# Three unused gaps in on-chip memory: moving every stationary operand of two MLP layers to the same place modulo 512 bytes

## The chip, the cores and the metric

The kernel runs on one core of a Trainium2 chip. The metric is device time in microseconds (us), and the figure given for a kernel is the median of its runs. A profile is one more execution, recorded by the hardware profiler; its time is its span, from the first instruction to the last.

The engines carry short names in the profile: PE is the matrix engine's multiplication, PEld its loading of weights (the stationary operand of a matmul, 128 rows by 128 columns, which must sit in the array before the moving operand, up to 512 columns, streams past it), DVE the vector engine, ACT the scalar engine, POOL the third elementwise engine, and SP the queue from which nearly all transfers (DMAs) are issued. SBUF is the on-chip memory of 128 partitions; an address below is the byte offset inside each partition.

## The reference: what is computed

Four layers are applied to x of 2048 tokens by 1024 channels, in float32: a convolution layer A, an MLP layer B, then A and B once more with the same weights.

```python
x = A_q
x = x + _A_ref(_layernorm(x), A_k, A_v, A_shift_k, A_ssm_k, A_ssm_D)
x = x + _B_ref(_layernorm(x), B_w1, B_b1, B_w2, B_b2)
x = x + _A_ref(_layernorm(x), A_k, A_v, A_shift_k, A_ssm_k, A_ssm_D)
x = x + _B_ref(_layernorm(x), B_w1, B_b1, B_w2, B_b2)
# _A_ref: k is convolved with 4 taps, multiplied by v, convolved causally with
#         a filter of 2048 taps per channel (by FFT in the reference), times q
# _B_ref: h = relu(x @ w1 + b1) ** 2      (1024 -> 3584)
#         h @ w2 + b2                     (3584 -> 1024)
```

The convolution's factor does not depend on x, so it is computed once and used in both A layers.

## The kernel before, in words

**Arithmetic.** An MLP product is made of three matmuls with operands split in a high and a low part (`mm3`, lines 334 to 337): high by high (L335), high by low (L336), low by high (L337), the first operand being the stationary one and the second the moving one. In the profile an instruction's inputs are named moving first: `p<-xh,whl` streams `xh` past weights `whl`.

**Tiling.** The 2048 tokens form 4 blocks of 512. A unit is one block in one MLP layer, eight in all, in the order of `ORDER`. Each unit has two kinds of matmul steps:

- m1 (first product): the stationary operand is a 128 by 128 piece of w1, in a tile `whl` (two parts of 512 columns), and the moving operand is the transposed, normalised block, `xh` and `xl`. A unit holds 28 hidden blocks of 128 by 8 input blocks by 3, which is 672 matmuls of 512 columns; at the seams of some units the block is taken in two halves of 256 columns.
- m2 (second product): the roles turn. The stationary operand is the activated hidden value, `rh` and `rl`, 128 of its 512 tokens at a time; the moving operand is a piece of w2 in `whl`. Units 0 to 4 have 28 hidden blocks by 2 halves of the output by 4 token tiles by 3, which is 672 such matmuls a unit.

In the last three units (`WINO`, units 5 to 7) the second product is done by a scheme with seven instead of eight products for each 2 by 2 group of blocks (4 token halves and weight blocks combined). Of its seven, three still take `rh` and `rl` as stationary operand (14 pairs by 3 by 2 by 3, 252 matmuls a unit), and four take sums of activations held in the tiles `cx`, `cg` (high parts), `cp`, `fy` (low parts) (14 by 4 by 2 by 3, 336 a unit). These four are called z below.

**Order of the work.** The order on each engine is written out by hand, step by step. Each step of the main loop (from `for s, (k, u, c, a, i, tts, w)` on) advances the ring of weights (`w_advance`: raw tiles `wr` loaded up to 8 steps ahead, the high part cast by ACT at L1012, the low part by DVE or POOL at L1020, or a split pair loaded ready-made from DRAM as `whl<-wd_m`), issues the matmuls, and then lets a share of the convolution's work (`prod_stream`, the product at L525 and its reduction at L529) and the preparation of the next unit run. The first block's convolution and normalisation are ordered ahead of that by a small planner (`first_block`). All of this depends on tiles and their buffers, not on addresses.

**Where the tiles lie.** Pools of SBUF lie end to end in the order in which they are opened: `const`, `cv`, `pre`, `mw`, `ml`. In a pool, names take their places in the order of first use, and each buffer is rounded up to a multiple of 32 bytes. This gives, for the kernel before:

| pool | tiles | byte address of the first | modulo 512 |
|---|---|---|---|
| const | ident, fh, fl, ih, il | 16512, then 17024, 19072, 21120, 22144 | 128 |
| cv | fx (4 buffers of 2080 bytes) | 23392 | 352, 384, 416, 448 |
| cv | yh, fg, cx, cg, cp, fk, sm, fy, yl | yh at 31712, cx at 41952, cp at 58336 | 480 |
| pre | px and small ones | px at 92096 | 448 (px) |
| mw | xh, xl, wr, whl | xh at 100736, whl at 149888 | 384 |
| ml | b1t | 174464 | 384 |
| ml | rh, rl, acc, yt | rh at 174592, rl at 190976 | 0 |

A 128 by 128 float32 piece takes 512 bytes of a partition, and the slices of `whl`, `rh`, `rl` and the z tiles start at whole multiples of 512 bytes within their tile. So in m1 stationary and moving operand both start at 384 modulo 512; in m2 the moving one starts at 384 and the stationary one at 0; in z it is 384 and 480. The prologue's pool `pro` lies where `ml` comes to lie later. The last byte used is at 227840.

Of the kernel before, what the change touches and what calls it, by code (L numbers as in the profile page):

```python
# [10 lines left out]
F32 = mybir.dt.float32  # L11
# [8 lines left out]
P = 128  # L20
# [4 lines left out]
FT = F // P  # L25
# [215 lines left out]
def tile_h3_mlp(ctx: ExitStack, tc: tile.TileContext, q, kT, vT, shk, ssmT, ssmD, w1, b1, w2, b2,  # L241
# [5 lines left out]
    dram = ctx.enter_context(tc.tile_pool(name="dram", bufs=1, space=DRAM))  # L247
    const = ctx.enter_context(tc.tile_pool(name="const", bufs=1))
    cv = ctx.enter_context(tc.tile_pool(name="cv", bufs=1))
    pre = ctx.enter_context(tc.tile_pool(name="pre", bufs=1))  # L250
    ps = ctx.enter_context(tc.tile_pool(name="ps", bufs=1, space=PSUM))
    ctx.enter_context(tc.manual_schedule())
# [800 lines left out]
            w_lo()  # L1053

    mw = ctx.enter_context(tc.tile_pool(name="mw", bufs=1))
    rs = {}

    def first_block():
# [423 lines left out]
    xT = first_block()  # L1482
    pds = prod_stream()
    ml = ctx.enter_context(tc.tile_pool(name="ml", bufs=1, reuse_waits="tile"))
    b1t = ml.tile([P, FT], F32, name="b1t", bufs=1)
    SY.dma_start(b1t, b1)
    lag = slag
    soon, behind = Later(), Later()
# [493 lines left out]
```

## Time and profile before

| | |
|---|---|
| three runs | 2735.21, 2728.89, 2734.58 us; median 2734.58 us |
| profiled execution, its span | 2729.8 us |
| granted PE clock in it, mean | 0.997 |
| PE busy | 2685.5 us, 98% |
| PE weight load busy | 2230.2 us, 82% |
| DVE / ACT / POOL busy | 1994.4 / 1124.3 / 844.6 us |
| DMA packets, share of 16 engines | 80.3% |

A busy time is the union of an engine's instructions. A matmul's record lasts longer than the distance to the next one's start, because matmuls are pipelined and their ends are modelled; so the mean duration of a record says less than the distance between starts. That distance is read from a stretch of time that holds only one kind of matmul: its length divided by their number. In a list of stretches, the number in brackets after a busy time counts every instruction that overlaps the stretch, so that one or two may reach in from before.

### The profile page before, as it was taken

The page shows a single profiled execution, that of the slowest core. Times are in us where ns is not written, and L with a number is a line of the kernel's source. Part 1 is how long each engine was busy: PE and PEld are TensorE (multiplying, and loading weights), DVE is VectorE, ACT ScalarE, POOL GpSimd, SP SyncE. Part 2 cuts the span into 40 slices and gives each one's busy share as a digit, 9 for nine tenths or more (in the row PEclk, how much of TensorE's full clock was granted, in tenths as well). Part 3 has the DMA queues.
Part 4 walks back from the last instruction along what each step waited for, and adds up shares of the span by engine and source line. Part 5 has one row for each costly group of instructions (what it writes and reads, how often), then busy time and mean ns, then how long its engine had stood idle before and what let it go on. Part 6 is the DMA issues. An engine that isn't in the chain of part 4 may idle for free.

```text
span 2729.8 us, 36533 instructions
## 1 busy us (share of the span) xinstructions
PE 2685.5 (98%) x12568; PEld 2230.2 (82%) x12568; DVE 1994.4 (73%) x3066; ACT 1124.3 (41%) x1936; POOL 844.6 (31%) x532
## 2 busy tenths in 40 slices
PE   7999999999999999999999999999999999999999
PEld 7888787888888888888888888888788788888887
DVE  7878888788987878779677655366787666664565
ACT  3454344434444233442234422244455444445443
POOL 2436564445532645236553454000100010001000
PEclk9999999999999999999999999999999999999999
DMA  7789898699989898888977887788888766685546
GB/s 251 263 299 318 288 316 290 213 312 374 322 297 326 293 338 276 273 330 286 348 259 270 300 296 251 228 287 311 304 281 299 275 230 212 223 282 198 177 166 204
DMA packets 377482, 755.05 MB, mean 277 GB/s; under 512 B 43840, under 2 KB 159184, under 8 KB 377296
## 3 DMA queue, kind: packets, MB, share of 16 engines
q1 hardware_dynamic: 377296, 752.72, 80.3%
q8 instruction: 99, 1.62, 0.3%
q14 instruction: 87, 0.71, 0.1%
HBM read 602.63 MB, written 149.95 MB: 276 GB/s over the span
## 4 chain that ended last, share of the span: by engine, by line
PE 80%; DMA 9%; DVE 5%; POOL 2%; issue 2%; SPq 1%; ACT 1%; DVEq 0%; POOLq 0%; ACTq 0%
PE p L336 24%; PE p L337 24%; PE p L335 24%; PE p L1095 2%; DMA wr<-w 2%; DMA cg<-gd 1%; DMA whl<-wd_m 1%; DVE whl L1020 1%; PE pt L335 1%; PE pt L337 1%; PE pt L336 1%; POOL cp L525 1%; DMA wd_m<-whl 1%; DMA wd_t<-whl 0%; DMA fg<-ssmT 0%
## 5 line engine op out<-in xcount | busy, mean ns | idle before, releaser
L525 POOL TENSOR_TENSOR cp<-cx,cg 128x384 f32<-128x384 f32 (+5 forms) x288 | 541.5, 1892 | 580.1 <-DVE sm L529 394.4
L335 PE MATMUL p<-xh,whl 128*128 128x512 f32 (+1 forms) x1840 | 706.7, 384 | 2.2 <-DMA whl<-wd_m 2.2
L337 PE MATMUL p<-xh,whl 128*128 128x512 f32 (+1 forms) x1840 | 703.5, 382 | 0.8 <-POOL whl L1020 0.8
L336 PE MATMUL p<-xl,whl 128*128 128x512 f32 (+1 forms) x1840 | 702.8, 382 | 0.1
L1012 ACT CAST whl<-wr 128x512 fp32r<-128x512 f32 x637 | 383.5, 619 | 445.9 <-PE p L337 270.2
L335 PE MATMUL p<-whl,rh 128*128 128x512 f32 x1372 | 548.1, 399 | 5.4 <-ACT whl L1012 3.6
L1020 DVE TENSOR_TENSOR whl<-wr,whl 128x512 fp32r<-128x512 f32 x622 | 499.4, 823 | 73.1 <-ACT whl L1012 65.0
L336 PE MATMUL p<-whl,rh 128*128 128x512 f32 x1372 | 543.8, 396 | 2.0 <-DVE whl L1020 1.1
L337 PE MATMUL p<-whl,rl 128*128 128x512 f32 x1372 | 543.0, 396 | 0.0
L335 PEld LDWEIGHTS p<-xh,whl 128*128 128x128 f32 x1840 | 346.2, 188 | 69.7 <-DVE acc L1606 1.8
L337 PEld LDWEIGHTS p<-xh,whl 128*128 128x128 f32 x1840 | 345.9, 188 | 68.7 <-POOL whl L1020 1.0
L336 PEld LDWEIGHTS p<-xl,whl 128*128 128x128 f32 x1840 | 346.0, 188 | 66.1 <-DVE xl L1408 0.3
L335 PEld LDWEIGHTS p<-whl,rh 128*128 128x128 f32 x1372 | 259.5, 189 | 65.8 <-ACT whl L1012 4.5
L336 PEld LDWEIGHTS p<-whl,rh 128*128 128x128 f32 x1372 | 259.6, 189 | 62.3 <-DVE whl L1020 3.3
L337 PEld LDWEIGHTS p<-whl,rl 128*128 128x128 f32 x1372 | 259.3, 189 | 60.5
L1502 DVE TENSOR_TENSOR rl<-wr,rh 128x512 fp32r<-128x512 f32 x140 | 143.3, 1024 | 181.6 <-ACT rh L1497 181.5
L1599 POOL TENSOR_TENSOR acc<-acc,px 128x512 f32<-128x512 f32 x18 | 23.1, 1321 | 771.2 <-DMA px<-b 771.2
L529 DVE TENSOR_REDUCE sm<-cp 128x128 f32<-128x384 f32 (+5 forms) x288 | 249.3, 874 | 9.3 <-POOL cp L525 9.3
L1494 ACT ACTIVATE wr<-p,b1t 128x512 f32<-128x512 f32 x138 | 95.3, 690 | 376.9 <-PE p L337 373.6
L1563 DVE TENSOR_TENSOR rl<-wr,rh 128x256 fp32r<-128x256 f32 x84 | 50.0, 596 | 209.4 <-ACT rh L1558 209.2
L1622 DVE TENSOR_TENSOR acc<-p,acc 128x512 f32<-128x512 f32 x152 | 101.5, 687 | 87.0 <-PE p L337 86.6
L1555 ACT ACTIVATE wr<-p,b1t 128x512 f32<-128x512 f32 x84 | 57.9, 689 | 189.8 <-PE p L337 187.9
(277 smaller groups left out, 3319.9 us busy)
## 6 DMA issues: line engine op xcount, KB each, us to landing
whl<-wd_m SPq DMA_DIRECT2D x379, 512.0 KB, 5.2
wr<-w SPq DMA_DIRECT2D x493, 256.0 KB, 5.3
wr<-td SPq DMA_DIRECT2D x152, 256.0 KB, 4.1
wd_m<-whl SPq DMA_DIRECT2D x70, 512.0 KB, 6.0
cx<-xd SPq DMA_DIRECT2D x48, 512.0 KB, 6.0
cg<-gd SPq DMA_DIRECT2D x48, 512.0 KB, 6.7
gd<-fg SPq DMA_DIRECT2D x72, 256.0 KB, 6.2
cx<-xd SPq DMA_DIRECT2D x48, 384.0 KB, 5.5
```

Source lines behind the costliest of these rows:

```text
L335: PE.matmul(o, lh, rh, start=start, stop=False)
L336: PE.matmul(o, lh, rl, start=False, stop=False)
L337: PE.matmul(o, ll, rh, start=False, stop=stop)
L525: G.tensor_mul(pr.rearrange("p c i -> p i c"), xt[:, 0:j + 1], gt[:, j::-1])
L529: V.tensor_reduce(sm[:, ty, jj], st["pr"], axis=AX.X, op=OP.add)
L1012: A.copy(t[:, 0], raws[n]["t"])
L1020: ENG[e[n % len(e)]].tensor_sub(t[:, 1], raws[n]["t"], t[:, 0].bitcast(F32))
L1095: PE.matmul(o, lh, r, start=start, stop=stop)
L1494: A.activation(r, st["o"], AF.Relu, bias=b1t[:, st["f"]:st["f"] + 1])
L1502: V.tensor_sub(st["lo"], st["r"]["t"], st["hi"].bitcast(F32))
L1555: A.activation(r, st["o"], AF.Relu, bias=b1t[:, st["f"]:st["f"] + 1])
L1622: V.tensor_add(accs[tt][:, d], o, accs[tt][:, d])
```

## The change

Three places take up room that nothing uses: a tile `gap` of 104 float32 (416 bytes) as the first of pool `cv`, a tile `gapm` of 24 float32 (96 bytes) as the first of pool `mw`, and 96 further float32 (384 bytes) behind `b1t`, the first tile of pool `ml`, which is then used through a slice of its old width.

```diff
     cv = ctx.enter_context(tc.tile_pool(name="cv", bufs=1))
+    cv.tile([P, 104], F32, name="gap", bufs=1)
     pre = ctx.enter_context(tc.tile_pool(name="pre", bufs=1))
...
     mw = ctx.enter_context(tc.tile_pool(name="mw", bufs=1))
+    mw.tile([P, 24], F32, name="gapm", bufs=1)
     rs = {}
...
     ml = ctx.enter_context(tc.tile_pool(name="ml", bufs=1, reuse_waits="tile"))
-    b1t = ml.tile([P, FT], F32, name="b1t", bufs=1)
+    b1t = ml.tile([P, FT + 96], F32, name="b1t", bufs=1)[:, 0:FT]
     SY.dma_start(b1t, b1)
```

The addresses follow. Pools `cv` and `pre` move up by 416 bytes: the `cv` tiles from 480 to 384 modulo 512, `fx` to 256, 288, 320 and 352, `px` to 352. Pool `mw` moves by 416 + 96 = 512 bytes and stays at 384. Pool `ml` begins 512 bytes higher, still at 384; `b1t` used to take 128 bytes and now takes 512 (496 rounded up), so `rh`, `rl`, `acc` and `yt` go from 0 to 384. After it the stationary and the moving operands of m1, m2 and z all start at 384 modulo 512. The last byte used is at 228736. No instruction, wait or transfer is added, removed or put elsewhere in the order.

## The prediction, on record before the result

> **What bounds the kernel now.** I read the page of the profile first: shares, slices, chain.
>
> ```profile
> span 2729.8 us, 36533 instructions
> PE 2685.5 (98%) x12568; PEld 2230.2 (82%) x12568; DVE 1994.4 (73%) x3066; ACT 1124.3 (41%) x1936; POOL 844.6 (31%) x532
> ...
> DMA  7789898699989898888977887788888766685546
> ...
> PE 80%; DMA 9%; DVE 5%; POOL 2%; issue 2%; SPq 1%; ACT 1%; DVEq 0%; POOLq 0%; ACTq 0%
> ```
>
> PE is busy for 98% of the span and carries 80% of the chain that ended last. A share of 98% still says nothing about how fast PE goes while busy, so I went on to the groups of PE instructions with shapes kept apart. The name before the comma is the moving operand, the one behind it the stationary one.
>
> ```profile
> L335 PE MATMUL p<-xh,whl 128*128 128x512 f32 x1712 | 670.0, 391 | 2.2 <-DMA whl<-wd_m 2.2
> L337 PE MATMUL p<-xh,whl 128*128 128x512 f32 x1712 | 667.1, 390 | 0.0
> L336 PE MATMUL p<-xl,whl 128*128 128x512 f32 x1712 | 666.5, 389 | 0.0
> L335 PE MATMUL p<-whl,rh 128*128 128x512 f32 x1372 | 548.1, 399 | 5.4 <-ACT whl L1012 3.6 <-DMA whl<-wd_m 1.6
> L336 PE MATMUL p<-whl,rh 128*128 128x512 f32 x1372 | 543.8, 396 | 2.0 <-DVE whl L1020 1.1 <-POOL whl L1020 0.9
> L337 PE MATMUL p<-whl,rl 128*128 128x512 f32 x1372 | 543.0, 396 | 0.0
> L337 PE MATMUL p<-whl,cp 128*128 128x512 f32 x264 | 104.6, 396 | 0.0
> L335 PE MATMUL p<-whl,cg 128*128 128x512 f32 x168 | 67.0, 399 | 0.3 <-DMA whl<-wd_t 0.3
> L335 PE MATMUL p<-whl,cx 128*128 128x512 f32 x168 | 66.8, 397 | 0.0
> L336 PE MATMUL p<-whl,cg 128*128 128x512 f32 x168 | 66.7, 397 | 0.3 <-DVE whl L1020 0.3
> L336 PE MATMUL p<-whl,cx 128*128 128x512 f32 x168 | 66.6, 396 | 0.0
> L337 PE MATMUL p<-whl,fy 128*128 128x512 f32 x72 | 28.5, 396 | 0.0
> ```
>
> All twelve groups are the same instruction: 128 rows by 128 columns, 512 columns moving. Yet m1 (the first three) lasts 389 to 391 ns and m2 and z last 396 to 399. The counts are m1 5136, m2 3 x 1372 = 4116, z 264 + 4 x 168 + 72 = 1008. The records overlap, so I look for the distance between starts. In the list of instructions in order of time I took the first matmul of a run of one kind and the first of the next kind, and in the list of stretches exactly what lies between:
>
> ```profile
> 1642.51 0.40 PE L335 MATMUL p<-whl,rh 128*128 128x512 f32 x1
> ...
> 1662.03 0.39 PE L335 MATMUL p<-xh,whl 128*128 128x512 f32 x1
> ...
> 2028.81 0.39 PE L335 MATMUL p<-whl,cx 128*128 128x512 f32 x1
> ...
> 2051.30 0.39 PE L335 MATMUL p<-xh,whl 128*128 128x512 f32 x1
> ...
> 2094.83 0.40 PE L335 MATMUL p<-whl,rh 128*128 128x512 f32 x1
> ```
>
> ```profile
> core 0: us, PE busy (x) PEld busy (x) DVE busy (x) ACT busy (x) POOL busy (x), PEclk, DMA share, GB/s
> 2051.30:2094.83 43.53, 43.53 (x193) 36.05 (x192) 32.34 (x68) 21.07 (x35) 0.00 (x0) 1.00 0.90 305
> 1642.51:1662.03 19.52, 19.52 (x86) 15.83 (x85) 16.76 (x18) 3.38 (x7) 14.92 (x8) 1.00 0.79 287
> 2028.81:2051.30 22.49, 22.49 (x97) 18.08 (x96) 17.41 (x32) 8.59 (x14) 0.00 (x0) 1.00 0.85 287
> ```
>
> By the code these stretches hold 8 hidden blocks of m1 (8 x 8 x 3 = 192 matmuls), one output half of seven hidden blocks of m2 (7 x 4 x 3 = 84), and four pairs of z (4 x 4 x 2 x 3 = 96). So a matmul takes 43.53 / 192 = 226.7 ns in m1, 19.52 / 84 = 232.4 ns in m2 and 22.49 / 96 = 234.3 ns in z, each with PE busy to the last hundredth and the granted clock at 1.00. No wait explains the difference; each rate is PE's own.
>
> What differs? m2 and z have the same moving tile `whl` and the same step of three matmuls, and still differ by 1.9 ns; what separates them is the stationary tile, at 0 modulo 512 in m2 and at 480 in z. m1 has it at 384, the place of its moving operand. Three places, three rates. The slices of `whl` and `rh` run through every multiple of 512 bytes, so a longer period than 512 is not what the rows ask for.
>
> **The change part by part.** No instruction is added, so every term is a change of duration.
>
> *The tiles `rh` and `rl` go from 0 to 384 (gap behind `b1t`).* If what sets the rate is the start of the stationary operand modulo 512, taken alone or against the moving operand at 384, m2 becomes what m1 is: 232.4 - 226.7 = 5.7 ns less, times 4116, 23.4 us. I take this value because m1's row is the nearest: the same instruction with both operands at 384. The other end is no gain, 0; a loss is weighed under the rivals.
>
> *The z tiles go from 480 to 384 (gap in `cv`).* 234.3 - 226.7 = 7.6 ns less, times 1008, 7.7 us; other end 0.
>
> *The gap in `mw`* gains nothing by itself: with the one in `cv` it makes 512 and keeps `whl`, `xh`, `xl` at 384. m1, 0 us.
>
> Sum if PE sets the end throughout: 31.1 us. How much of it reaches the end is seen from PE's idle time by region:
>
> ```profile
> 0.00:546.00 546.00, 512.45 (x2730) 441.60 (x2731) 447.58 (x686) 238.38 (x422) 258.89 (x202) 0.98 0.84 280
> 546.00:1843.00 1297.00, 1294.67 (x6000) 1073.26 (x5999) 972.49 (x1338) 471.04 (x831) 555.06 (x307) 1.00 0.86 298
> 1843.00:2729.80 886.80, 878.39 (x3842) 715.34 (x3840) 574.31 (x1044) 414.86 (x684) 30.61 (x24) 1.00 0.71 243
> 570.00:720.00 150.00, 148.50 (x703) 123.89 (x702) 135.01 (x170) 58.83 (x106) 84.66 (x50) 1.00 1.00 351
> ```
>
> Up to 546 us (prologue and unit 0, with 672 m2) PE is idle for 33.6 us: others end there. Of unit 0's 672 x 5.7 = 3.8 us I count half, because I cannot say which of its steps wait; the bounds are 0 and 3.8. From 546 to 1843 us (units 1 to 4, 2688 m2, 15.3 us of gain) PE is idle for 2.3 us in 1297, so the gain goes through. The one warning is 570 to 720 us, where the DMA share is 1.00: there transfers cannot come any faster, and about 150 / 1297 of 2688 m2, 311 of them worth 1.8 us, may give half of it back. From 1843 us on (756 m2 worth 4.3 us, z worth 7.7 us) PE is idle for 8.4 us of 887 and the DMA share is 0.71: all of it counts. The cover for the rest is DVE, whose busy share between 546 and 1843 us is 972 / 1297 = 75%; 1.2% less time makes it 76%. If that cover were gone, the 15.3 us would be. The stretch with the least room is again 570 to 720 us, DVE 135 of 150.
>
> So 31.1 - 1.9 - 0.9 = 28.3 us.
>
> *What else moves.* These rows price it.
>
> ```profile
> L335 PE MATMUL p<-xh,whl 128*128 128x256 f32 x128 | 36.7, 287 | 0.0
> L335 PE MATMUL pt<-fg,fh 128*128 128x256 f32 x64 | 18.2, 284 | 1.5 <-DVE fy L403 1.5
> L336 PE MATMUL pt<-fx,fh 128*128 128x256 f32 x64 | 18.0, 281 | 0.0
> L1012 ACT CAST whl<-wr 128x512 fp32r<-128x512 f32 x637 | 383.5, 619 | 445.9 <-PE p L337 270.2 <-DMA wr<-w 46.3 <-DVE acc L1606 34.9
> L1497 ACT CAST rh<-wr 128x512 fp32r<-128x512 f32 x140 | 87.0, 622 | 4.5
> acc<-x SPq DMA_DIRECT2D x25, 512.0 KB, 7.2
> px<-x SPq DMA_DIRECT2D x32, 512.0 KB, 6.0
> ```
>
> The convolution's matmuls of 256 columns (576 of them, stationary `fh`, `fl`, `ih`, `il` at 128) see their moving tiles go from 480 (or `fx`, 352 to 448) to 384 (256 to 352). The known rows of this shape lie between 281 and 287 ns at three pairs of places, so each may change by 6 ns either way: 576 x 6 = 3.5 us, either sign. I take 0, as the two nearest rows differ by 3 ns without an order. ACT's cast to 384 (619 ns) and to 0 (622) agree within 3 ns, and ACT has room, so 0. DMAs: `acc` at 0 lands 7.2 us after its issue, `px` at 448 after 6.0, for the same 512 KB; the position at 0 has no advantage to lose, 0. Were transfers to `acc` and `yt` slower after all, they are issued some steps ahead of use and their cover is the m1 work in between.
>
> [...]
>
> **The profile against the runs.** The sum is made against the profiled span of 2729.8 us: 2729.8 - 28.3 = 2701.5. The median of the runs is 2734.6, 4.8 us above that span, and I carry this over: 2706.3, rounded to 2706.
>
> **The rivals.**
>
> *Others keep the pace (partial).* From 546 to 1843 us DMA (share 0.86, in places 1.00) and DVE give the whole gain of units 1 to 4 back as waits of PE. Against it: PE's 2.3 us of idle time there show no near limit. What is left is 4.3 + 7.7 = 12 us: 2723.
>
> *Place does nothing.* m2 and z are slow because `whl` is their moving operand (it is rewritten all the time, `xh` is not) or because their output bank changes every three matmuls. Then the time stays at 2735. For it: m1 alone has `xh` as moving operand, so the trace never shows m2 at 384. Against it: z and m2 share both traits and differ. [...]
>
> *The wrong place (slower).* In m1 the stationary tile is `whl`; the pair of `whl` moving past an `rh` or z tile that starts at the same 384 occurs nowhere in the trace. If equal places collide for this pair, the price may be both known costs together, 5.7 + 7.6 = 13.3 ns over 226.7, 240.0 ns for all 5124 matmuls: 4116 x 7.6 + 1008 x 5.7 = 37 us, 2772. It decides from the present mean on, (4116 x 232.4 + 1008 x 234.3) / 5124 = 232.8 ns; above it the kernel is slower. Against it: m1 runs at equal places in 5136 matmuls, without a trace of a collision.
>
> **How the numbers follow.** About 0.3%, 8.2 us, is what a measurement of this kernel can tell from no change. The forecast (m2 and z at m1's rate) has 0.80; the partial gain 0.07; no effect 0.08; slower 0.05. The first two are faster by more than 0.3%: faster 0.87, same 0.08, slower 0.05. The range: the full 31.1 us and the 3.5 us of the convolution's matmuls give 2734.6 - 34.6 = 2700, and 2 us less for the spread of a median of three; the upper end takes in the partial rival at 2723. 2698 to 2723 leaves out no effect and slower, 0.13, and little of the rest.
>
> **What would show it.** Right: m2's and z's groups at 389 to 391 ns like m1's; a stretch of 84 m2 in 19.04 us and of 96 z in 21.8 us, with m1's 192 still in 43.5; PE's busy time down by about 29 us with its idle time hardly larger; DVE, ACT, POOL and DMA with the same busy time in a shorter span. Wrong by the partial rival: the same new rates, but PE idle time grown by 10 us or more between 546 and 1843 us, put down to `whl` or its transfers. Wrong by place doing nothing: the same 232.4 and 234.3. Wrong by collision: m2 and z above 234. What would also make it wrong is a change to m1 at 226.7, since all its 5136 matmuls hang on one rate: each ns there is 5 us.

## The result, and the profile after

The changed kernel takes 2710.68 us (median of five runs, 2707.62 to 2713.36) against 2730.33 us for the kernel before (five runs, 2728.01 to 2735.21). The ratio is 0.9925, with a 95% interval of 0.9913 to 0.9937: about 20 us, 0.75%, faster. Measured a second time beside other kernels it came out at 0.9918 (0.9906 to 0.9931). The forecast was 2706 us, a gain of 28.3 us; the direction and the range held, and about 8 us of the gain did not arrive. (The median of before fell by 4 us when two more runs joined the first three. The forecast had carried the higher median over, so in absolute time it misses by 4 us only.)

The page of the changed kernel, first its span, busy times and chain. Line numbers in its profile are one higher than before from line 250 on, and two higher from line 1057 on, because of the two added lines.

```profile
span 2708.9 us, 36533 instructions
...
PE 2658.2 (98%) x12568; PEld 2227.5 (82%) x12568; DVE 1988.0 (73%) x3066; ACT 1124.1 (41%) x1936; POOL 845.8 (31%) x532
...
PE 82%; DMA 7%; DVE 6%; issue 2%; POOL 1%; ACT 1%; SPq 1%; DVEq 0%; ACTq 0%; POOLq 0%
```

The number of instructions is the same on every engine. PE's busy time fell by 27.3 us (a fall of about 29 was one of the forecast's signs), and the other engines kept theirs within 6.4 us. The span fell by 20.9 us only, so PE's idle time grew, from 44.3 to 50.7 us.

The groups of PE instructions, shapes kept apart (m1, m2 and z, one or two rows of each):

```profile
L336 PE MATMUL p<-xh,whl 128*128 128x512 f32 x1712 | 670.8, 392 | 4.3 <-DMA whl<-wd_m 4.2
L338 PE MATMUL p<-xh,whl 128*128 128x512 f32 x1712 | 667.5, 390 | 0.0
L337 PE MATMUL p<-whl,rh 128*128 128x512 f32 x1372 | 536.6, 391 | 1.8 <-POOL whl L1021 0.8 <-DVE whl L1021 0.8
L338 PE MATMUL p<-whl,rl 128*128 128x512 f32 x1372 | 536.0, 391 | 0.0
L338 PE MATMUL p<-whl,cp 128*128 128x512 f32 x264 | 102.8, 389 | 0.0
```

And the stretches that answer to those of before: 192 matmuls of m1, 84 of m2, 96 of z, each from the first matmul of a run to the first of the next.

```profile
2035.49:2079.01 43.52, 43.52 (x193) 36.05 (x192) 32.28 (x68) 21.06 (x35) 0.00 (x0) 1.00 0.90 308
1629.11:1648.15 19.04, 19.04 (x86) 15.77 (x84) 14.73 (x18) 3.38 (x7) 14.72 (x8) 1.00 0.85 295
2013.73:2035.49 21.76, 21.76 (x97) 18.02 (x96) 17.50 (x32) 8.61 (x14) 0.00 (x0) 1.00 0.87 290
```

43.52 / 192, 19.04 / 84 and 21.76 / 96 are all 226.7 ns. m1 has kept its rate, and m2 (232.4 before) and z (234.3 before) have taken it on. What was forecast of PE's pace came true in these stretches to a tenth of a nanosecond; what went missing is to be looked for elsewhere, in waits and in the clock.

PE's idle time by region, with the borders moved to where the same matmuls stand:

```profile
0.00:546.00 546.00, 508.63 (x2734) 441.35 (x2735) 449.53 (x686) 238.11 (x423) 259.58 (x202) 0.98 0.85 280
546.00:1830.00 1284.00, 1282.44 (x6010) 1073.76 (x6009) 968.20 (x1344) 471.29 (x831) 555.09 (x307) 1.00 0.87 302
1830.00:2708.90 878.90, 867.15 (x3828) 712.43 (x3826) 570.26 (x1037) 414.72 (x683) 31.15 (x24) 1.00 0.72 244
```

In the first 546 us PE's busy time is 3.8 us less, about the gain of unit 0's 672 matmuls, and its idle time 3.8 us more; at 546 us the changed kernel is 4 matmuls ahead (2734 against 2730), less than 1 us. In the middle 1284 us now hold 6010 matmuls where 1297 us held 6000: 13.0 us plus ten matmuls of 0.22 is 15.2 us. In the last region 7.9 us are gained with 14 matmuls fewer, 4.7 us in all, and the idle time grew from 8.4 to 11.8 us. So the first region gave about 1 us, units 1 to 4 gave 15.2, units 5 to 7 gave 4.7: 20.9 together. This split is that of one profile of each kernel, and it is not firm: in a second profile of the changed kernel (`after_again`, below) the starts of the same matmuls give -1.4, 11.9 and 7.5 us (0.5, 15.6 and 4.7 in the first).

### The profile page after: what moved, and what is told of

It reads as the page before. It is cut to its first block, busy times and chain, and to the rows that moved or that the text cites. A ratio compares the mean times of both kernels' runs of the same rounds, so it can differ in the third digit from the quotient of the medians.

```text
span 2708.9 us, 36533 instructions
## 1 busy us (share of the span) xinstructions
PE 2658.2 (98%) x12568; PEld 2227.5 (82%) x12568; DVE 1988.0 (73%) x3066; ACT 1124.1 (41%) x1936; POOL 845.8 (31%) x532
## 4 chain that ended last, share of the span: by engine, by line
PE 82%; DMA 7%; DVE 6%; issue 2%; POOL 1%; ACT 1%; SPq 1%; DVEq 0%; ACTq 0%; POOLq 0%
PE p L336 25%; PE p L337 25%; PE p L338 25%; DMA wr<-w 2%; PE p L1097 2%; DVE whl L1021 1%; DMA whl<-wd_m 1%; PE pt L336 1%; PE pt L337 1%; PE pt L338 1%; DMA wd_m<-whl 1%; DMA whl<-wd_t 1%; DMA yt<-yd 0%; DMA wd_t<-whl 0%; DMA fx<-kT 0%
## 5 line engine op out<-in xcount | busy, mean ns | idle before, releaser
L336 PE MATMUL p<-whl,rh 128*128 128x512 f32 x1372 | 541.2, 394 | 7.3 <-ACT whl L1013 3.7
L337 PE MATMUL p<-whl,rh 128*128 128x512 f32 x1372 | 536.6, 391 | 1.8 <-POOL whl L1021 0.8
L338 PE MATMUL p<-whl,rl 128*128 128x512 f32 x1372 | 536.0, 391 | 0.0
```

Of the source, the lines that this page charges most:

```text
L336: PE.matmul(o, lh, rh, start=start, stop=False)
L337: PE.matmul(o, lh, rl, start=False, stop=False)
L338: PE.matmul(o, ll, rh, start=False, stop=stop)
```

## The experiments

### Each gap alone: `rh_only` and `z_only`

```diff
# rh_only
-    b1t = ml.tile([P, FT], F32, name="b1t", bufs=1)
+    b1t = ml.tile([P, FT + 96], F32, name="b1t", bufs=1)[:, 0:FT]
# z_only
+    cv.tile([P, 104], F32, name="gap", bufs=1)
...
+    mw.tile([P, 24], F32, name="gapm", bufs=1)
```

> Only the gap behind b1t: rh and rl at 384 modulo 512, z tiles left at 480. If the place of the stationary operand against the moving one sets the rate, m2 falls from 232.4 to 226.7 ns and z stays at 234.3. Of the 23.4 us on PE, unit 0's 3.8 us and some of the last units' 4.3 us go into waits: 13 to 17 us faster than before. If m2 was slow for its moving tile or its output banks, m2 stays at 232.4 and the time at 2730. If both gaps were needed together, nothing moves here.

> Only the gaps in cv and mw (416 and 96 bytes): z tiles at 384, rh and rl left at 0. By the place theory z falls from 234.3 to 226.7 ns and m2 stays at 232.4; 7.7 us on PE, of which waits at the seams of the last three units take some: 4 to 7 us faster. If the two gains add up, this and the run with rh alone sum to the 19.7 us of the whole change. If place does nothing, 0.

`rh_only`: 2714.13 us, ratio 0.9943 (0.9930 to 0.9955), 15.6 us faster. `z_only`: 2724.20 us, ratio 0.9975 (0.9966 to 0.9984), 6.8 us faster. The sum of the two, 22.4 us, is the whole change within the intervals. Stretches of `rh_only`, 84 of m2 and 96 of z:

```profile
1628.21:1647.25 19.04, 19.04 (x86) 15.77 (x84) 14.75 (x18) 3.38 (x7) 14.94 (x8) 1.00 0.83 295
2010.53:2033.02 22.49, 22.49 (x98) 18.08 (x96) 17.54 (x32) 8.29 (x14) 0.00 (x0) 1.00 0.85 287
```

The same two kinds in `z_only`:

```profile
1638.77:1658.28 19.51, 19.51 (x85) 15.83 (x84) 16.74 (x18) 3.37 (x7) 14.89 (x8) 1.00 0.81 289
2026.92:2048.70 21.78, 21.78 (x98) 18.02 (x96) 17.36 (x32) 8.38 (x14) 0.00 (x0) 1.00 0.86 282
```

In `rh_only` m2 runs at 226.7 ns and z still at 234.3; in `z_only` m2 is at 232.3 and z at 226.9. Each rate follows the place of its own stationary operand, also where the other's stays; the rival that m2 and z are slow for their moving tile or their output banks is gone. Both times lie in the ranges expected, 13 to 17 and 4 to 7 us.

### Own place or distance: `x_moved` and `all_zero`

The prediction left open whether 384 is a good place or whether being at the moving operand's place is what counts.

```diff
# x_moved: xh, xl at 480; whl, rh, rl and z tiles at 384
+    cv.tile([P, 104], F32, name="gap", bufs=1)
+    mw.tile([P, 48], F32, name="gapm", bufs=1)
-            big = {nm: new(mw, nm, 1, [P, KT * T]) for nm in ("xh", "xl")}
+            big = {nm: new(mw, nm, 1, [P, KT * T + n]) for nm, n in (("xh", 0), ("xl", 104))}
+    b1t = ml.tile([P, FT + 96], F32, name="b1t", bufs=1)[:, 0:FT]
# all_zero: gaps of 8, 24 and 96 float32 put all of them at 0
```

> All as in the changed kernel, but xh and xl, the moving operand of m1, start at 480 modulo 512, with every stationary operand still at 384. Relative theory (the distance between the two operands counts): m1 leaves 226.7 ns and takes 5.7 to 7.6 ns more, 29 to 39 us slower than the changed kernel, 2740 to 2750, while m2 and z stay at 226.7. Absolute theory (the stationary operand's own place counts, 384 is good): m1 stays at 226.7 and the time is that of the changed kernel, 2711.

> Gaps of other sizes put moving and stationary operands of m1, m2 and z all at 0 modulo 512. Relative theory: all three at 226.7 ns, the time of the changed kernel, 2711. Absolute theory (0 costs what m2 paid before): m1, m2 and z all at about 232.4 ns; against before, m1 adds 5136 x 5.7 = 29 us and z gives 2 us: about 2757.

`x_moved`: 2736.84 us, ratio to before 1.0021 (1.0012 to 1.0031), that is 1.0021 / 0.9925 = 1.0097 of the changed kernel, about 26 us slower. `all_zero`: 2707.33 us, ratio 0.9917 (0.9903 to 0.9931), the changed kernel's time. The 192 matmuls of m1 in `x_moved`:

```profile
2051.07:2095.88 44.81, 44.81 (x193) 36.05 (x192) 32.44 (x68) 20.94 (x35) 0.00 (x0) 1.00 0.88 300
```

m1, m2 and z in `all_zero`:

```profile
2038.50:2082.02 43.52, 43.52 (x193) 36.04 (x192) 32.27 (x68) 21.06 (x35) 0.00 (x0) 1.00 0.90 308
1631.63:1650.67 19.04, 19.04 (x85) 15.77 (x84) 16.68 (x18) 3.38 (x7) 14.86 (x8) 1.00 0.83 293
2016.74:2038.50 21.76, 21.76 (x97) 18.02 (x96) 17.48 (x32) 8.67 (x14) 0.00 (x0) 1.00 0.85 289
```

With its stationary operand unmoved and its moving operand 96 bytes away, m1 takes 44.81 / 192 = 233.4 ns. At 0 everything runs at 226.7 ns, the very place at which m2 used to take 232.4 with its moving operand at 384. So neither of these two places is good or bad by itself; the distance between the two operands is what counts. The 26 us of `x_moved` are less than the 5136 x 6.7 = 34 us by PE and than the 29 to 39 expected. Between the profiles of the two kernels PE's busy time grew by 29.8 us (2658.2 to 2688.0) while its idle time fell by 5.6 (50.7 to 45.1): here waits absorbed 5.6 us of a loss, as they absorbed 6.4 us of the gain (44.3 to 50.7). The mean granted clock differs too, 0.998 against 0.996.

The matmuls of 256 columns don't show the effect at 96 bytes. At the seams, m1 runs with 256 columns moving. 96 of these, in the changed kernel and then in `x_moved`:

```profile
505.64:517.16 11.52, 11.52 (x98) 11.51 (x97) 10.23 (x25) 4.94 (x8) 3.41 (x3) 1.00 0.89 311
504.59:516.11 11.52, 11.52 (x97) 11.52 (x96) 10.23 (x25) 4.95 (x8) 3.42 (x3) 1.00 0.85 309
```

Both are 120 ns a matmul, at equal starts and 96 bytes apart. The loading of weights (PEld, the third number) is busy here for all of the 11.5 us, against 36.05 of 43.52 us in the stretch of 512 columns.

### Other distances: `near` and `far`

```diff
# near: rh, rl 32 bytes past the moving operand, z tiles 64
+    cv.tile([P, 120], F32, ...)   mw.tile([P, 8], F32, ...)    b1t: FT + 108
# far: rh, rl 256 past it, z tiles 384
+    cv.tile([P, 72], F32, ...)    mw.tile([P, 56], F32, ...)   b1t: FT + 36
```

> Gaps of other sizes: moving operands at 384, rh and rl at 416 (32 bytes past them), z tiles at 448 (64 past them). Known so far: 0 past costs nothing over 226.7 ns, 96 past 7.6, 128 past 5.7. If the cost rises smoothly with the distance, m2 at about 229 and z at about 232 ns; if anything but equality costs about the same, m2 and z at 232 to 235 and the time about 2728; if the cost starts only where the distance passes 64 bytes, both at 226.7 and the time that of the changed kernel, 2711.

> Moving operands at 384, rh and rl at 128 (256 past them, modulo 512), z tiles at 256 (384 past them). If only equality is cheap, m2 and z again cost 5 to 8 ns more than 226.7 and the time is within 10 us of before. If half of 512 is as good as 0, m2 is at 226.7 and the time about 2715. If the cost grows with distance, m2 is above 234 and the kernel slower than before.

`near`: 2733.87 us, ratio 1.0007 (0.9997 to 1.0017), not to be told from before and 6 us above the 2728 expected. `far`: 2713.73 us (two runs), ratio 0.9932 (0.9914 to 0.9950). m2 and z in `near`:

```profile
1645.94:1665.53 19.59, 19.59 (x85) 15.77 (x84) 16.73 (x18) 3.38 (x7) 14.90 (x8) 1.00 0.82 286
2032.76:2055.16 22.40, 22.40 (x97) 18.05 (x96) 17.38 (x32) 8.30 (x14) 0.00 (x0) 1.00 0.84 283
```

m2 and z in `far`:

```profile
1627.36:1646.39 19.03, 19.03 (x85) 15.76 (x84) 16.67 (x18) 3.38 (x7) 14.92 (x8) 1.00 0.82 292
2013.02:2035.34 22.32, 22.32 (x98) 18.09 (x97) 17.55 (x32) 8.70 (x14) 0.00 (x0) 1.00 0.84 291
```

| stationary minus moving start, modulo 512 | 0 | 32 | 64 | 96 | 128 | 256 | 384 | 416 |
|---|---|---|---|---|---|---|---|---|
| ns from start to start | 226.7 | 233.2 | 233.3 | 234.3 | 232.4 | 226.5 | 232.5 | 233.4 |
| measured on | m1, m2, z, changed kernel | m2, `near` | z, `near` | z, before | m2, before | m2, `far` | z, `far` | m1, `x_moved` |

The cost doesn't rise with distance; of the eight distances two are cheap, 0 and 256, and the rest cost 5.7 to 7.6 ns. A distance of 384 costs what 128 does. So the rows fit a period of 256 bytes, and not the 512 of the change's name; two pairs of distances (0 and 256, 128 and 384) show it. `rh` and `rl` would have done as well 256 bytes further on: `far`, which leaves z slow at 232.5 ns, gains about what `rh_only` does.

### Where the rest of the gain went: the bias and its two buffers

In the last units the longest wait of PE sits near 1906 us. Stretches of 5 us around it in the changed kernel, then the queue's and PE's longest waits there:

```profile
1894.00:1899.00 5.00, 5.00 (x24) 4.14 (x23) 1.05 (x1) 1.32 (x3) 5.00 (x5) 1.00 0.97 356
1899.00:1904.00 5.00, 5.00 (x23) 4.14 (x23) 3.58 (x6) 1.47 (x4) 3.37 (x3) 1.00 0.27 84
1904.00:1909.00 5.00, 2.47 (x11) 1.70 (x10) 4.90 (x11) 2.49 (x4) 0.00 (x0) 1.00 0.92 287
1909.00:1914.00 5.00, 4.73 (x14) 3.74 (x15) 0.66 (x2) 0.10 (x1) 0.00 (x0) 0.66 0.93 339
```

```profile
SPq L726 <- POOL fk L1601: 8.1, 1, 8.1
...
PE p L336 <- DMA whl<-wd_m: 2.8, 1, 2.8
```

To be read in order: the queue SP stands still for 8.1 us at a load into `px`, whose buffer POOL is still reading for the second bias (`add_b2w`); the transfer engines, full until then (0.97), run dry (0.27); the weights behind that load come 2.8 us late; and after PE's pause the granted clock is 0.66 in a stretch of 5 us. Eight matmuls, from 1910.31 us on, take 0.37 to 0.43 us from start to start there in place of 0.23, and over these 3.35 us the mean clock is 0.51. So this is half speed for 3.4 us, which costs 1.7 us. The pause alone doesn't bring it on: `after_again` below has a longer one, 3.5 against 2.8 us, without it. The kernel before has the same standstill, with shorter waits behind it:

```profile
SPq L725 <- POOL fk L1599: 7.8, 1, 7.8
...
PE p L335 <- DMA whl<-wd_m: 1.2, 2, 0.9
```

I shifted the bias, first earlier and then later, in both kernels.

```diff
# b2early: 34 -> 18, 38 -> 22     b2late: 34 -> 38, 38 -> 40
-                lag.at(34, load_b2, bst)
-                lag.at(38, add_b2w, bst, wacc)
+                lag.at(18, load_b2, bst)
+                lag.at(22, add_b2w, bst, wacc)
```

> The kernel before, with the load of the second bias and its addition (on POOL) 16 steps earlier in the last three units, ahead of the loads that use the same two buffers. Theory of the queue: SP stands still for 7.8 us behind those additions, and the weight loads behind it come late; with them earlier, PE's waits of 1.1 and 0.4 us at 1923 and 1933 us go: 1 to 2 us faster, 2729. Theory of the full transfer queue: the waits come from the amount of data, and nothing changes.

> The same edit on the changed kernel. Theory of the queue: the wait of 2.8 us at 1906 us goes, and with it the half clock of 3.4 us that follows it (1.7 us lost): 3 to 5 us faster than the changed kernel, about 2706, so that the whole change is worth 23 us in place of 20. Theory of the full transfer queue: no change, 2711. In both the waits at 2118 and 2413 us, which lie at the ends of units, stay.

`before_b2early`: 2744.73 us, ratio 1.0049 (1.0035 to 1.0063). `after_b2early`: 2722.66 us, 0.9966 (0.9953 to 0.9978). Both are 11 to 13 us slower than without the edit. SP's wait for POOL is gone, but another one took its place; from the list of waits of `after_b2early`, last three units:

```profile
DVE acc L1608 <- POOL acc L1601: 11.4, 5, 4.9
```

The additions now fall in the time when DVE evicts into the same accumulators; DVE waits for POOL, the weights' low parts behind it are late (PE waits 8.6 us for DVE's, against 0.8 in the changed kernel), and PE stops in the z steps.

> The kernel before, with the second bias loaded 4 steps later and added 2 steps later in the last three units: behind the last load that uses the same two buffers, and ahead of the evictions into the same accumulators. Theory of the queue: SP no longer waits for POOL, PE's waits at 1923 and 1933 us go, no new wait on DVE comes up: 1 to 2 us faster than before. Theory of the full transfer queue: no change.

> The same edit on the changed kernel. Theory of the queue: the wait of about 3 us at 1906 us and the half clock behind it go, 3 to 5 us faster than the changed kernel, so that the step from the kernel before (with the same edit) is 22 to 24 us. Theory of the full transfer queue: the time of the changed kernel, and the same waits.

`before_b2late`: 2738.07 us, ratio 1.0021 (1.0012 to 1.0029). `after_b2late`: 2714.66 us, 0.9937 (0.9925 to 0.9949). Slower again than without the edit, by 4 to 6 us. From `after_b2late`, the queue's wait and a stretch of 5 us:

```profile
SPq L1740 <- DVE mv L698: 11.3, 1, 11.3
```

```profile
1895.00:1900.00 5.00, 5.00 (x24) 4.13 (x22) 3.36 (x8) 2.56 (x5) 0.00 (x0) 1.00 0.01 3
```

Now it is the bias's load that stands in the queue, for 11.3 us, until DVE has read the statistics' input out of the same two buffers; the transfers fall to a share of 0.01 and PE's wait grows to 3.4 us. My claim that these shifts would free the queue was wrong: they moved the conflict over the two `px` buffers, they did not remove it.

> The changed kernel itself, beside the two others on one chip. If the wait of 2.8 us at 1906 us with its half clock belongs to the kernel, this profile shows it again, as two other kernels with fast z did (z alone, and all at 0). If it was chance, it is absent. The time: 2711, 0.9925 of before.

`after_again`, the changed kernel unedited: 2710.68 us, ratio 0.9918. SP again waits 9.0 us for POOL, and PE's longest wait for `whl<-wd_m` is 3.5 us, at the same matmul; so the wait belongs to the kernel. The half clock does not. It was expected too, and the stretches in which PE pauses and goes on have the full clock:

```profile
1909.00:1914.00 5.00, 3.09 (x14) 2.24 (x12) 4.93 (x11) 2.67 (x4) 0.00 (x0) 1.00 0.67 219
1914.00:1919.00 5.00, 3.44 (x15) 2.77 (x16) 1.90 (x5) 0.39 (x1) 0.00 (x0) 1.00 1.01 375
```

In this profile the clock halves for 3.4 us near 1508 us instead, where the other profile has it full.

Last, I took away what SP waited for: the other user of the two buffers begins later.

```diff
-            if n == 28:
+            if n == (44 if u in WINO else 28):
                 pa = prep_a(*ORDER[u + 1])
-            elif n > 28 and pa is not None and next(pa, 0) == 0:
+            elif pa is not None and next(pa, 0) == 0:
```

> The changed kernel, with the four loads for the next unit's statistics (line 726, tile px) begun 16 steps later in the last three units, after the bias in the same two buffers has been used up. The two shifted biases each put another wait in the place of the one on POOL, so this takes away what makes SP wait there. If SP's standstill is what empties the transfer queue and makes PE wait at 1906 us: SP's 18 us behind POOL go, the stretch with a DMA share of 0.3 fills up, PE's wait of 2.8 us and the half clock behind it go, 3 to 5 us faster than the changed kernel, 2706 to 2708. If the loads, now in the z steps, hold SP there instead: PE's wait moves to z and the time is 2711 or more. If the full queue before the hole is the cause, the wait stays.

`after_later_x`: 2708.05 us, ratio 0.9911 (0.9895 to 0.9928). The same stretches, and PE's longest waits in the last three units:

```profile
1894.00:1899.00 5.00, 5.00 (x24) 4.14 (x23) 0.51 (x1) 1.56 (x3) 5.00 (x5) 1.00 1.08 389
1899.00:1904.00 5.00, 5.00 (x24) 4.14 (x23) 4.11 (x8) 2.59 (x4) 0.41 (x1) 1.00 0.97 358
1904.00:1909.00 5.00, 5.00 (x24) 4.14 (x23) 1.19 (x3) 1.29 (x4) 0.00 (x0) 1.00 1.02 372
```

```profile
PE p L337 <- DVE whl L1021: 3.6, 9, 0.8
PE p L336 <- DMA whl<-wd_m: 3.5, 5, 1.0
```

The hole is filled (0.27 became 0.97), PE is busy throughout, its wait for `whl<-wd_m` in these units fell from 7.2 to 3.5 us, and no half clock follows there. So the standstill of SP on the `px` buffers is what made PE wait at 1906 us; the longer standstill of `b2late` (11.3 us), with PE's wait of 3.4 to 3.5 us in both kernels, agrees. The edit also takes a load of 512 KB away from in front of the weights, and its share isn't separated. But 3.6 us of waits for the weights' low parts on DVE came up in their stead, where the statistics now fall among the z steps, and SP now waits 14.6 us for DVE at the same load (`SPq L726`). The median is 2.6 us below the changed kernel's, and the intervals overlap: not shown to be faster.

## Why the prediction was right, and where it was off

**Rates.** m2 to m1's rate and z to m1's rate: right, to the tenth of a nanosecond in the stretches shown, and m1 unmoved. The prediction argued from three places and three rates; that the relation of the two operands and not the place sets the rate was left open there and is shown by `x_moved` and `all_zero`. That a period longer than 512 isn't asked for was right; 256 fits the distances tried.

**The rivals.** Place does nothing: ruled out by each gap alone, which took m2 from 232.4 to 226.7 ns and z from 234.3 to 226.9. The wrong place: `whl` moving past `rh` at an equal place runs at 226.7 ns, no collision. Others keep the pace in units 1 to 4: no, these gave 15.2 us, and 11.9 in the second profile, where it would have been none.

**Units 1 to 4.** 15.3 us were counted, less 0.9 for the stretch with a DMA share of 1.00. 15.2 us came in the first profile, so that the reserve was not needed there. That this hits the count so well is partly luck: in the second profile 11.9 came, with 2.9 us lost near 1505 us, where the clock halved. That transfers cannot come faster at a share of 1.00 was an estimate: that stretch moved 351 GB/s, and 5 us of the kernel before, from 1930 us on, 410 at 1.05.

**Unit 0.** Half of 3.8 us was counted; about 1 us or less arrived, and PE's idle time grew by 3.8 us. That fits the reading that PE waits for others here and a faster PE only waits longer; no run tests it.

**Units 5 to 7: the step that failed.** "From 1843 us on [...] all of it counts" sized this term at 12 us, and 4.7 arrived (7.5 in the second profile). The reasons given were small idle time and a DMA share of 0.71. Both are means over 887 us. In the stretches of 5 us the same region has shares of 1.0 next to 0.27, from a queue that stands still; a PE that arrives earlier there waits, 2.8 us at the longest near 1906 us against 0.9 before. From the starts of the same matmuls in the two profiles, the stretch around 1906 us (80 matmuls of m1) took 2.7 us longer than before, and the two ends of units near 2118 and 2413 us 0.9 and 1.0 us longer. The remaining 2.7 us lie in many small delays. In the second profile the stretch around the wait is again 1.8 us longer, while the two ends together are not: of the three, only the wait at 1906 us recurs. `after_later_x` shows its cause.

Why this wait is longer in the changed kernel than before, with standstills of 8.1 and 7.8 us, is half settled. The last of POOL's eight additions, which SP waits for, sorts the nine profiles that have bias and loads in their old places. It takes 1.73 us in the six where PE waits 1.9 us or more here (the changed kernel twice, `z_only`, `all_zero`, `far`, `x_moved`), and 1.29 us in the three where PE waits 0.9 us or less (before, `rh_only`, `near`). The last two additions before and after:

```profile
1916.15 2.54 POOL L1599 TENSOR_TENSOR fk<-fk,px 128x512 f32<-128x512 f32 x2
...
1899.38 2.99 POOL L1601 TENSOR_TENSOR fk<-fk,px 128x512 f32<-128x512 f32 x2
```

In the six, a subtraction of DVE (`rl<-wr,rh`) starts 0.2 to 0.9 us ahead of that addition; in the three it starts with it or up to 0.2 us behind it. So the long waits go with a fraction of a microsecond in the order of two engines. The longer addition ends SP's standstill 0.4 us later; that the weights behind it also land later, 6.4 us after their issue against about 5.3, stays open, and no run tests this reading.

**Costed at nothing.** Rightly: the convolution's matmuls took 69.0 us from start to start against 70.6 before, 1.5 us of the difference being one wait for DVE (`fy`) in the profile before; `acc<-x` lands after 7.3 us (7.2 before) and `px<-x` after 6.2 (6.0).

## What to carry to other kernels

When two groups of the same matmul instruction differ in rate with no wait between, compare the start addresses of the stationary and the moving operand: in this kernel equal starts modulo 256 bytes gave 226.5 to 226.7 ns a matmul, and every other distance tried 232 to 234, and some hundred bytes of padding moved all into the first class. With 256 columns moving, tried at 96 bytes, there was nothing to gain (120 ns both times). A gain on the busiest engine did not arrive in full here, 20 us of 28.3, and part of it was lost where a queue stood still for 8.1 us: look for holes in the transfers at a scale of a few us, not at the mean share of a region, and take a second profile before you trust the split by region. A wait in a queue that comes from two users of one pair of buffers (8.1 us) moved in both shifts of one user here, to waits of 11.4 us on DVE and 11.3 us in the queue; shifting the other removed it, and brought other waits of about the same size (3.6 us of PE's for DVE, where 3.7 for the weights had gone).

## What the runs showed of the hardware that was not expected

The spacing of these 512-column matmuls depends on the distance between stationary and moving operand: 226.7 ns at 0, 226.5 at 256, 232.4 to 234.3 at 32, 64, 96, 128, 384 and 416, which fits a period of 256 bytes. At a distance of 0 it is the same for three pairs of tiles and at two places in SBUF (384 and 0 modulo 512); each other distance was measured with one pair of tiles. With 256 columns moving, 120 ns a matmul, a distance of 96 bytes costs nothing. Why the spacing depends on the distance, no run shows.

Where an addition of POOL and a subtraction of DVE overlap at the bias, one of the two was longer: in the changed kernel the addition took 1.73 us and the subtraction 0.84, before it was 1.29 and 1.79. Where the subtraction starts 0.2 us or more ahead (six profiles), the addition takes 1.73 us in place of 1.29. Where it doesn't (three profiles), the subtraction takes 1.6 to 1.9 us in place of the 0.80 to 0.91 of those that start 0.2 to 0.3 us ahead.
